# One scale for each head pair of batch 0, a weight bound from maxima, and two results moved from PSUM to SBUF, with the instruction order laid anew

## The chip, the cores and the metric

The kernel runs on one core of one Trainium2 chip. The metric is the time of one execution on the device, in microseconds. Five engines of the core appear here: PE (TensorE, the matrix engine; PEld are its weight loads), DVE (VectorE), ACT (ScalarE), POOL (GpSimd) and SP (SyncE, which here only starts DMA transfers). Each engine works through its own instructions strictly in the order of the program; the engines wait for one another by semaphores. SBUF is the on-chip memory that all engines and the DMA engines reach; matmuls write to PSUM.

## The reference

Eight batches, each of 576 tokens, go through three stages. Stage 1 is attention over 8 heads of 64, masked by blocks of 64 tokens. Stage 2 is a mixture of four attention experts, of which each token takes two. Stage 3 is a gated MLP that mixes tokens with a 576 x 576 matrix.

```python
scores = q @ k.T / 8;  scores = where(block_i >= block_j, scores, -1e9)
attn = exp(scores - max);  attn = attn / (sum(attn) + 1e-9)
x = concat_heads(attn @ v)                              # 8 x 576 x 512, fp32

logits = x @ w_gate;  topk, w = two best of 4, softmax of their logits
for e in range(4):                                      # causal attention of each expert
    ye = softmax(causal(x @ wq[e] @ (x @ wk[e]).T / 8)) @ (x @ wv[e]) @ wo[e]
    out += where(e in topk, w_e, 0) * ye

h = relu(out @ w_in);  u, v = halves of h (512 each)
v_n = (v - mean) / sqrt(var + 1e-6)
result = (u * (w_spatial @ v_n + b_spatial)) @ w_out
```

All inputs are fp32. The kernel keeps fp32 accuracy with 16-bit matmuls: every operand is scaled by a power of two, split into a high and a low fp16 part, and each product is three matmuls (high x high, high x low, low x high).

## The kernel before

**Tiles and steps.** Heads are taken in pairs: four pairs per batch in stage 1 and two pairs of experts (numbers 4 and 5) in stage 2, so 48 pairs in all. Everything that belongs to a pair or a batch is cut into *steps*, and each step into pieces that run on one engine each. For a pair of stage 1: the loads of q and k, and of v, into a buffer `nat` (load_qk, load_v); the maxima of their absolute values (mags, L279 or L281); the transposes and the split into fp16 (prep_qk L320, split16 L227 and L233; prep_v). One scale per batch comes from the maxima of all four pairs (scale1, scale2; col_max L195, bcast L206, scales L213 to L222). For every pair: four blocks of scores (matmuls L369, last block L384), each followed by the row maximum (L391, L393), a small step that makes the bias of the exponential from it (L401 on ScalarE or L403 on VectorE), and the exponential (L407, L412). The exponentials of blocks 0 to 2 land in SBUF buffers `pf`; that of the last block, 576 columns, is written back into its own PSUM buffer. Then the weights are split: a 16-bit copy (L327, L329 or L331) and a subtraction (L431) that gives the low part. They are transposed by three DMA transposes (L438, weights_t), and attention x V follows (av, L448). Its result is divided by the row sums (L464 to L466) and multiplied in place in PSUM (L471); a cast (L480 or L482) and a subtraction (L484), both from PSUM, give its two 16-bit halves `xh`, which a DMA transposes (L486).

The six pairs of a batch feed the dense part: projections (proj L803), vproj (L826), gate, then the two expert pairs, then hv (L882), norm (L920 to L926), gating (L961), gating2 (L977 to L985) and outp (L997, L1000).

**Buffers.** PSUM is four buffers called `duo`, 1024 fp32 columns each, and every step that uses TensorE takes one. A buffer comes free when the last piece that reads it is done. `pf` has three buffers, `nat` four.

**Startup.** Beside batch 0 the weights are prepared. w_in and w_out come as 64-bit words (s_win, s_wout, conversion L511 to L531) and are split (s_hl L714, L716). Of wq, wk and wv a bound on their column sums is taken: absolute values on ScalarE (L597), then 16 fp32 matmuls with a matrix of ones (s_abm, L626). The constants that follow from it (s_cons, L633 to L656) are needed before the dense part, and the steps of all weights of a pair wait for that bound. w_spatial is loaded into the buffers `pT` and transposed from there (L675).

**What sets the order.** Nothing is scheduled at run time. A list of numbers, ORDER, says which step runs its next piece, and a table, WAYS, says on which engine a piece runs that several engines can do ("AG": copy on ScalarE, subtraction on GpSimd). A piece may only come after the pieces it depends on and after its buffers are free, and each engine then meets its instructions in the order of the list.

## Time and profile before

| | |
|---|---|
| median of 3 runs | 1085.67 us (1085.58, 1085.67, 1089.9) |
| span of the profiled execution | 1086.0 us |
| TensorE busy | 894.5 us (82%) |
| VectorE busy | 832.3 us (77%) |
| ScalarE busy | 666.3 us (61%) |
| GpSimd busy | 374.6 us (34%) |
| DMA queue 1, which SyncE starts | 134.03 MB, 67.2% of 16 engines' span |

The profile is that of one execution. Each engine has a line that says how long it was busy; "idle before" an instruction is the time in which its engine had nothing to run, and the name behind the arrow is what ended it. PEclk is the clock that was granted to TensorE, as a share of its full 2.4 GHz; the DMA share is the mean busy share of the core's 16 DMA engines.

### The profile page before, as it was taken

Reading aid. Unit: us, or ns where it says so; the run is one execution under the profiler, and the core shown is the slowest. Engines: PE = TensorE matmul, PEld = TensorE weight load, DVE = VectorE, ACT = ScalarE, POOL = GpSimd, SP = SyncE. Lnnn points to the kernel's source line nnn. Section 1 sums busy time; section 2 is a strip of 40 time slices with the busy share of each in tenths; the row PEclk is TensorE's granted clock in tenths of the full one; section 3 lists DMA queues with packets and bytes.
Section 4 is the critical chain, followed back from the end, with each engine's and each line's share of the span. In section 5 each row is a group of like instructions: output and inputs, shape, how many; then the busy total and the mean of one; then the engine's idle time right before and its main releaser. Section 6 shows DMA issues by size and latency. Waiting matters only on the chain.

```text
span 1086.0 us, 25340 instructions
## 1 busy us (share of the span) xinstructions
PE 894.5 (82%) x10170; PEld 649.8 (60%) x10170; DVE 832.3 (77%) x1719; ACT 666.3 (61%) x1154; POOL 374.6 (34%) x307
## 2 busy tenths in 40 slices
PE   0477677777889799599999888987999999999978
PEld 0255555656567467466676556755777677667644
DVE  2698889898976868877897889877987887657550
ACT  2758467586677646666567657865667774636432
POOL 5145504152154212343244414354564044305000
PEclk9968687988989899799999998998999999999989
DMA  9536989798379678559649994959968546923601
GB/s 221 135 84 142 188 150 179 147 163 148 80 128 177 132 146 158 105 116 184 129 94 172 177 171 97 163 118 200 142 103 138 131 70 113 191 61 55 130 8 44
DMA packets 496663, 143.68 MB, mean 132 GB/s; under 512 B 484288, under 2 KB 490608, under 8 KB 496544
## 3 DMA queue, kind: packets, MB, share of 16 engines
q1 hardware_dynamic: 483744, 134.03, 67.2%
q0 software_dynamic: 2336, 5.55, 1.9%
q10 hardware_dynamic: 10464, 2.47, 1.4%
q8 instruction: 80, 1.31, 0.5%
q14 instruction: 39, 0.32, 0.1%
HBM read 38.19 MB, written 9.44 MB: 44 GB/s over the span
## 4 chain that ended last, share of the span: by engine, by line
PE 33%; DVE 14%; DMA 7%; ACT 6%; issue 4%; SPq 2%; POOL 1%; DVEq 0%; ACTq 0%; POOLq 0%
PE duo L977 7%; PE duo L997 6%; PE duo L448 5%; DMA pT<-p 5%; PE duo L803 4%; PE duo L369 3%; ACT pf L412 2%; PE duo L961 2%; DVE st L391 2%; PE duo L882 2%; PE duo L826 2%; PE duo L320 1%; DMA nat<-in_k_dram 1%; PE duo L384 1%; DMA nat<-in_v_dram 1%
## 5 line engine op out<-in xcount | busy, mean ns | idle before, releaser
L431 POOL TENSOR_TENSOR p<-pf,p 128x1024 f16<-128x1024 f32 (+1 forms) x96 | 187.3, 1954 | 326.3 <-ACT p L327 217.2
L412 ACT ACTIVATE pf<-duo,st,es 128x128 f32<-128x128 f32 (+3 forms) x256 | 139.3, 621 | 65.0 <-DVE st L403 48.1
L448 PEld LDWEIGHTS <-pT 128*128 128x128 f16 x4320 | 151.4, 101 | 29.9 <-issue 12.1
L391 DVE TENSOR_REDUCE st<-duo 128x2 f32<-128x1024 f32 (+1 forms) x192 | 150.8, 813 | 14.6 <-PE duo L377 8.4
L369 PE MATMUL duo<-qk 64*128 64x256 f16 (+3 forms) x1152 | 117.6, 321 | 29.7 <-ACT pf L412 14.0
L977 PE MATMUL duo<-wsp,vn 128*128 128x288 f16 x896 | 121.7, 290 | 11.2 <-ACT vn L923 5.5
L448 PE MATMUL duo<-v,pT 128*128 128x65 f16 (+1 forms) x2880 | 108.9, 200 | 15.0 <-DMA pT<-p 7.1
L997 PE MATMUL duo<-wo,gT 128*128 128x512 f16 (+1 forms) x480 | 109.2, 383 | 8.5 <-DVE xh L484 3.9
L977 PEld LDWEIGHTS <-vn 128*128 128x128 f16 x896 | 87.1, 99 | 36.2 <-ACT vn L923 6.1
L803 PE MATMUL duo<-x,wqk 128*128 128x288 f16 x768 | 102.4, 294 | 5.6 <-ACT pf L412 2.0
L803 PEld LDWEIGHTS <-wqk 128*128 128x128 f16 x768 | 76.2, 100 | 27.8 <-issue 6.3
L369 PEld LDWEIGHTS <-qk 64*128 64x128 f16 x1152 | 49.9, 99 | 62.1 <-issue 44.0
L997 PEld LDWEIGHTS <-gT 128*128 128x128 f16 (+1 forms) x480 | 47.2, 101 | 62.5 <-issue 12.3
L281 DVE TENSOR_REDUCE mst<-nat 128x1 f32<-128x640 f32 (+1 forms) x52 | 55.4, 1069 | 35.5 <-DMA nat<-in_v_dram 26.8
L412 ACT ACTIVATE pf<-duo,st,mt 128x384 f32<-128x384 f32 (+3 forms) x128 | 69.9, 616 | 15.0 <-DVE st L403 12.1
L331 POOL TENSOR_SCALAR p<-pf 128x1024 f16<-128x1024 f32 (+1 forms) x36 | 36.5, 1014 | 117.3 <-DMA pT<-p 62.6
L327 ACT CAST p<-pf 128x1024 f16<-128x1024 f32 (+1 forms) x71 | 66.5, 947 | 9.1 <-DMA pT<-p 7.1
L320 PE MATMUL duo<-ident,nat 128*128 128x128 f32 (+1 forms) x320 | 56.4, 314 | 17.1 <-DVE xh L484 6.4
L826 PE MATMUL duo<-wvg,x 128*128 128x260 f16 x480 | 57.6, 278 | 11.6 <-DVE st L403 5.8
L233 DVE SCALAR_TENSOR_TENSOR qk<-duo,scb,qk 128x640 f16<-128x640 f32 (+1 forms) x64 | 52.7, 843 | 18.4 <-ACT qk L227 18.2
L227 ACT ACTIVATE qk<-duo,scb 128x640 f16<-128x640 f32 (+1 forms) x64 | 47.8, 769 | 25.9 <-PE duo L320 15.9
L384 PE MATMUL duo<-qk 128*128 128x288 f16 x288 | 47.6, 303 | 17.5 <-ACT pf L412 13.2
(257 smaller groups left out, 1740.1 us busy)
## 6 DMA issues: line engine op xcount, KB each, us to landing
out_dram<-o SPq DMA_DIRECT2D x16, 512.0 KB, 3.3
nat<-in_q_dram SPq DMA_DIRECT2D x54, 128.0 KB, 3.1
nat<-in_k_dram SPq DMA_DIRECT2D x54, 128.0 KB, 3.1
nat<-in_v_dram SPq DMA_DIRECT2D x54, 128.0 KB, 3.1
wf<-in_moe_w_in_dram SPq DMA_DIRECT2D x8, 512.0 KB, 4.6
pT<-p SPq DMA_TRANSPOSE x144, 4.9
wf<-in_moe_w_out_dram SPq DMA_DIRECT2D x4, 512.0 KB, 4.9
nat<-in_q_dram POOLq DMA_DIRECT2D x10, 128.0 KB, 4.6
```

What stands on the lines that cost most here:

```text
L320: T.transpose(ps[:, P * c:P * c + r], p.nat[0:r, i, c, :], ident[0:r, 0:r])
L327: A.copy(hi, src)
L369: T.matmul(ph[:, hh, o:o + w], p.q[hs, a, ts], p.k[hs, bb, 0:w], start=i == 0, stop=False)
L384: T.matmul(ps[:, MID + a:MID + a + n], p.q[:, l, 512:640], p.k[:, r, a:a + n], start=i == 0, stop=i == 2 and not (p.moe and a))
L391: V.reduce_max(st[:, 0, 2 * c:2 * c + 2], ph[:, :, off[c]:off[c] + P * (c + 1)], axis=AX.X)
L412: A.activation(pf[:, n * hh + off[c]:n * hh + off[c] + w], ph[:, hh, off[c]:off[c] + w], AF.Exp, bias=st[:, 1, 2 * c + hh:2 * c + hh + 1], ...
L431: (V if way[1] == "D" else G).tensor_sub(lo, src, hi)
L448: T.matmul(ps[:, hh, o:o + n], pT[:, col(t, kk):col(t, kk) + P], p.v[:, hh, kk, a:a + n], start=kk == 0 and i == 0, stop=kk == nk - 1 and ...
L803: T.matmul(ps[:, MID + a:MID + a + w], wqk16[:, l, c, 2 * n + i, :], x16[c][:, r, a:a + w], start=m == 0, stop=m == 11)
L826: T.matmul(ps[:, i, :260], x16[d][:, l, P * c:P * c + P], wvg16[:, r, d, :], start=m == 0, stop=m == 11)
L977: T.matmul(ps[:, MID + a:MID + a + n], vn[:, l, ds_], wsp16[:, r, c, a:a + n], start=i == 0, stop=False)
L997: T.matmul(ps[0:r, i], gT[:, x, d, P * c:P * c + r], wo16[:, y, d, :], start=m == 0, stop=m == 11)
```

## The change

- **Start.** The buffers `nat` are made first, and GpSimd's first instruction clears the part of them that no load fills. The table of the exponential is loaded on ScalarE by one dummy instruction. The padding of `p16` and `pT` is cleared once, so one small matmul per pair (before at the end of scores) goes.
- **Batch 0** takes a scale of its own for each head pair (scale0, and scale2 with n = 2), from that pair's q and k alone; v still has one scale per batch.
- **Weight bound.** Absolute values and the matmuls of s_abm go; the bound comes from the largest element of the weights (s_mxA), which the scale of the weights needs in any case. The weights steps of pairs no longer wait for it. w_spatial is loaded into tiles of its own.
- **Last exponential** goes to a fourth `pf` buffer in SBUF, and its PSUM buffer is free after it. Copy and subtraction of that block read SBUF and may run on any engine.
- **Attention output** is multiplied from PSUM into a `pf` buffer (halves, first piece), and PSUM is free after that. Cast and subtraction read SBUF; the subtraction may run on GpSimd.
- **Attention x V** starts with the first of the three transposes and waits for each as it comes to it.
- **ORDER and WAYS** are new. All conversions and splits of w_in and w_out run on GpSimd, more bias steps on ScalarE, 40 of 48 subtractions of the attention output on GpSimd; of the 48 subtractions of the last block 37 stay on VectorE.

```diff
-BIG = -1.0e38
+BIG = -1.0e35
...
+    nat_t = buffers("nat", 4, 3 * NC * P).rearrange("p n (i c d) -> p n i c d", i=3, c=NC)
+    G.memset(nat_t[:, 0, :, 4], 0.0)
...
-    buffers("pf", 3, 1024)
+    buffers("pf", 4, 1024)
...
+    A.activation(junk[:, 0:1], ones[:, 0:1], AF.Exp)
...
+    def scale0(b, pr):
+        s = BS[b].own[pr]
+        s.dg = yield from col_max(duo(), s.st[:, :, 0], 2, "o")
...
     def prep_qk(b, pr, i):
         p, s = PD[b, pr], BS[b]
+        if b == 0:
+            s = s.own[pr]
...
-            T.matmul(ps[:, MID + S:MID + 640], identb, m_row[:, 64:128], start=True, stop=True)
...
-            A.activation(ps[:, MID:MID + S], ps[:, MID:MID + S], AF.Exp, bias=st[:, 1, 8:9], scale=p.es)
+            A.activation(pf[:, 0:S], ps[:, MID:MID + S], AF.Exp, bias=st[:, 1, 8:9], scale=p.es)
...
-        V.tensor_mul(ov[:, :, :, 0:64], ov[:, :, :, 0:64], r.unsqueeze(3).to_broadcast([P, 2, NC, D]))
-        p.x32 = ov[:, :, :, 0:64]
+        p.ov, p.r = ov[:, :, :, 0:64], r
     def halves(p, way):
...
-        if way == "A":
-            A.copy(hh, p.x32)
-        else:
-            V.tensor_copy(hh, p.x32)
-        yield
-        V.tensor_sub(hl, p.x32, hh)
+        x = mine("pf")[:, 0:640]
+        V.tensor_mul(x.rearrange("p (c h d) -> p h c d", h=2, c=NC), p.ov,
+                     p.r.unsqueeze(3).to_broadcast([P, 2, NC, D]))
+        yield
+        copy16(h[:, 0], x, way[0])
+        yield
+        (V if way[1] == "D" else G).tensor_sub(h[:, 1], x, h[:, 0])
...
-        def s_absA():
-            A.activation(t["aqk"], t["wqk"].rearrange("p c g i e d -> p c (g i e d)"), AF.Abs, accum_out=t["st"][:, 0:1])
...
+        def s_mxA(i):
+            V.tensor_reduce(t["st"][:, i:i + 1], (t["wqk"].rearrange("p c g i e d -> p (c g i e d)"),
+                                                  t["wv"].rearrange("p c e d -> p (c e d)"))[i],
+                            op=OP.max, axis=AX.X, apply_absolute_value=True)
...
-        def s_abm(i):
-            for c in range(KD):
-                T.matmul(pb[:, :n], ones, t[a][:, c, :], start=c == 0, stop=c == KD - 1)
-            V.reduce_max(t["amax"][:, i:i + 1], pb[:, :n], axis=AX.X)
...
     ORDER = (
...
-        "su.win.0": ("D",), "su.hl.0": ("D",), "su.win.1": ("G",), "su.hl.1": ("G",), "su.win.2": ("D",),
+        "su.win.0": ("G",), "su.win.1": ("G",), "su.win.2": ("G",), "su.win.3": ("G",), "su.win.4": ("G",),
...
+        "x.0": ("AG", "AG", "AG", "AG", "AG", "GD", "AG", "GD"), "x.1": ("AG", "AG", "DG", "AD", "AG"),
```

Three places show how the instructions move. The first is TensorE at the start of the program. Before, in a row (`p` holds absolute values of weights, `wst` and `m` maxima, L320 transposes the first pair's q):

```order
L626 MATMUL duo<-p_140,ones 128x256 x4
L626 MATMUL duo<-p_140,ones 128x512 x4
L195 MATMUL duo<-ident,m_318 3x128
L195 MATMUL duo<-ident,wst 5x128
L700 MATMUL duo<-ident,V_144 128x128 x8
L206 MATMUL duo<-dgb,ones 128x3
L206 MATMUL duo<-dgw,ones 128x5
L320 MATMUL duo<-ident,nat 128x128 x9
L320 MATMUL duo<-ident,nat 128x64
```

After, the same engine from its first instruction to its first scores:

```order
L199 MATMUL duo<-ident,mst_217 2x128
L210 MATMUL duo<-dgo,ones 128x2
L343 MATMUL duo<-ident,nat 128x128 x9
L343 MATMUL duo<-ident,nat 128x64
L389 LDWEIGHTS qk
L389 MATMUL duo<-qk 128x512
```

The weight bound, the weights' scale and w_o's transposes no longer stand ahead of the first pair; two small matmuls of the pair's own scale do.

The second place is VectorE in the middle of the program, at the end of a pair's attention. Before (`rr` is the reciprocal of the row sums, `xh` the halves of the attention output, L980 a step of the gated MLP):

```order
L464 TENSOR_SCALAR rr<-duo 128x10
L466 RECIPROCAL rr<-rr 128x10
L471 TENSOR_TENSOR duo<-duo,rr 128x2x5x64
L484 TENSOR_TENSOR xh<-duo,xh 128x2x5x64
L980 TENSOR_TENSOR u<-duo,u 128x576
```

After, at such a place:

```order
L480 TENSOR_SCALAR rr<-duo 128x10
L482 RECIPROCAL rr<-rr 128x10
L485 TENSOR_TENSOR rr<-rr,wt 128x10
L410 TENSOR_REDUCE st<-duo 128x2 x3
L493 TENSOR_TENSOR pf<-duo,rr 128x2x5x64
L448 TENSOR_TENSOR p_144<-pf,p_144 128x1024
L352 CAST p_144<-pf 128x1024
```

The subtraction has left VectorE here, and the multiplication is what frees the PSUM buffer.

The third place is GpSimd, where those subtractions (L498) now stand among the weights' (L448), after:

```order
L448 TENSOR_TENSOR p_144<-pf,p_144 128x1024 x2
L498 TENSOR_TENSOR xh<-pf,xh 128x640
L448 TENSOR_TENSOR p_144<-pf,p_144 128x1024
L498 TENSOR_TENSOR xh<-pf,xh 128x640
L448 TENSOR_TENSOR p_144<-pf,p_144 128x1024
L354 TENSOR_SCALAR xh<-pf 128x640
L448 TENSOR_TENSOR p_144<-pf,p_144 128x1024
L498 TENSOR_TENSOR xh<-pf,xh 128x640
```

Before, GpSimd had no instruction on `xh`; now a weight subtraction stands ahead of most of them.

## Rows read from the trace of the kernel before

**Rows 1.** Busy time, share of the span and instruction count of each engine.
```profile
PE 894.5 (82%) x10170; PEld 649.8 (60%) x10170; DVE 832.3 (77%) x1719; ACT 666.3 (61%) x1154; POOL 374.6 (34%) x307
```

**Rows 2.** Stretches: length, each engine's busy time (instructions), PEclk, DMA share, GB/s.
```profile
0.00:66.00 66.00, 18.55 (x71) 12.26 (x72) 33.97 (x97) 33.22 (x58) 27.06 (x52) 0.90 0.77 166
66.00:240.00 174.00, 124.19 (x1445) 97.79 (x1446) 157.35 (x278) 116.58 (x211) 62.95 (x42) 0.79 0.82 152
240.00:955.00 715.00, 635.13 (x7708) 462.92 (x7703) 574.85 (x1189) 465.32 (x801) 265.30 (x196) 0.96 0.76 139
955.00:1086.00 131.00, 116.64 (x956) 76.87 (x953) 66.11 (x156) 51.20 (x85) 19.32 (x17) 0.94 0.24 53
...
100.00:140.00 40.00, 26.81 (x324) 22.85 (x323) 34.13 (x54) 23.74 (x43) 18.41 (x11) 0.70 0.91 159
850.00:900.00 50.00, 48.41 (x475) 35.07 (x474) 41.64 (x99) 36.75 (x70) 13.29 (x12) 1.00 0.49 94
```

**Rows 3.** Timeline of PE: start, length, instruction, in brackets the idle time before it.
```profile
36.69 8.19 PE L626 MATMUL duo<-p,ones 128*128 128x256 f32 x16 [36.69 <-ACT p L597]
...
65.99 1.64 PE L369 MATMUL duo<-qk 64*128 64x512 f16 x6
...
240.42 0.91 PE L384 MATMUL duo<-qk 128*128 128x288 f16 x6
...
954.90 1.39 PE L803 MATMUL duo<-x,wqk 128*128 128x288 f16 x5
```

**Rows 4.** Timeline of POOL, SP (its DMA issues) and ACT at the start.
```profile
5.28 1.49 POOL L162 MEMSET nat<- 128x384 f32 x4
...
9.22 1.21 SPq L254 DMA_DIRECT2D nat<-in_q_dram  x2
10.47 0.66 SPq L256 DMA_DIRECT2D nat<-in_k_dram  x1
...
17.33 1.28 ACT L279 ACT_TABLE_LOAD   x1 [17.33 <-DMA nat<-in_k_dram]
```

**Rows 5.** Waits of PE, 240 to 955 us: engine, line, releaser; total us, times, longest.
```profile
PE duo L384 <- ACT pf L412: 8.1, 6, 3.7
PE duo L320 <- DVE xh L484: 6.4, 2, 3.8
...
PE duo L997 <- DVE xh L484: 3.9, 1, 3.9
...
PE duo L448 <- DVE xh L484: 2.1, 2, 1.1
...
PE duo L206 <- ACT pf L412: 0.5, 1, 0.5
```

**Rows 6.** DVE groups, 0 to 240 us: instruction, shape, count; busy us, mean ns; idle before.
```profile
L431 DVE TENSOR_TENSOR p<-pf,p 128x1024 f16<-128x1024 f32 x9 | 12.1, 1349 | 1.9 <-POOL p L331 1.9
...
L281 DVE TENSOR_REDUCE mst<-nat 128x2 f32<-128x1280 f32 x5 | 7.4, 1485 | 1.2 <-DMA nat<-in_k_dram 1.1
...
L484 DVE TENSOR_TENSOR xh<-duo,xh 128x640 f16<-128x640 f32 x7 | 5.7, 813 | 0.0
...
L530 DVE TENSOR_TENSOR x<-x,e 128x512 f32<-128x512 f32 x5 | 3.4, 685 | 0.1
...
L403 DVE TENSOR_SCALAR st<-st,es 128x2 f32<-128x2 f32 x9 | 2.3, 255 | 0.0
```

**Rows 7.** Single lines over the span: count, shortest/median/longest in ns, first to last, shapes.
```profile
L431 DVE TENSOR_TENSOR p<-duo,p x48: 802/815/825, 84.6 to 1010.8; 128x640 f16<-128x640 f32 x48
...
L985 DVE TENSOR_TENSOR gT<-u,gT x13: 744/749/2203, 343.1 to 1069.4; 128x576 f16<-128x576 f32 x13
...
L431 POOL TENSOR_TENSOR p<-pf,p x96: 1150/2128/3186, 76.3 to 998.9; 128x1024 f16<-128x1024 f32 x72, 128x512 f16<-128x512 f32 x24
```

**Rows 8.** ACT groups over the whole span, columns as in rows 6.
```profile
L480 ACT CAST xh<-duo 128x640 f16<-128x640 f32 x44 | 30.6, 695 | 25.1 <-DVE duo L471 15.7 <-PE duo L379 4.3 <-issue 2.9
...
L401 ACT ACTIVATE st<-st,ln,es 128x2 f32<-128x2 f32 x20 | 7.7, 387 | 18.1 <-DVE st L391 18.1
```

More of the change, by code (lines that the diff above doesn't have):

```diff
@@ L101, in attn_moe_gmlp_kernel @@
     onesb = cst.tile([P, P], BF, name="onesb")
+    for n in range(1, 4):
+        G.memset(nat_t[:, n, :, 4], 0.0)
     G.memset(onesb, 1.0)
@@ L160, in attn_moe_gmlp_kernel @@
     junk = cst.tile([P, 640], BF, name="junk")
-    for n in range(4):
-        G.memset(nat_t[:, n, :, 4], 0.0)
     for n in range(3):
@@ L353, in scores @@
             p.st = sm.tile([P, 2, 9], F32, name="st")
[L354 to L358 removed]
+            p.pf, p.p16, p.pT = {}, {}, {}
+        pf = p.pf[j] = mine("pf")
         st = p.st
@@ L424, in weights @@
             p.p16[g] = mine("p16")
-        s0, n, o0, per = WCOL[j]
-        src = p.pf[j][:, s0:s0 + n] if j < 3 else p.last[:, s0:s0 + n]
+        n, o0, per = WCOL[j]
+        src = p.pf[j][:, 0:n]
         t = p.p16[g]
@@ L1370, in pair_steps @@
         for j in range(4):
[L1371 to L1375 removed]
+            n = (1024, 1024, 512, 576)[j]
```

162 lines of the change are left out of this document (80 added, 82 removed), and 475 rows, old and new, of tables (ORDER, WAYS).

## The prediction

> **What bounds the kernel now.** I read the busy times first [rows 1]. TensorE is busy for 894.5 us of 1086.0, VectorE for 832.3, ScalarE for 666.3, GpSimd for 374.6: no engine is full, so the question is where TensorE waits. The stretches of [rows 2] answer it. The borders are points that the reordered program passes too: 66 us is the first score matmul, 240 us the last score block of batch 0's second expert pair, 955 us the first projection of batch 7 [rows 3]. In the first 66 us TensorE works for 18.6 us. From 66 to 240 it works for 124.2 of 174, at a granted clock of 0.79, and VectorE is busy for 157.4, that is 90%: VectorE sets the pace there. The DMA share is 0.82, so it is second. From 240 to 955 TensorE works for 635.1 of 715 at clock 0.96, and VectorE for 574.9 (80%): TensorE leads, with 79.9 us of idle time. The last 131 us are batch 7's own chain, with no other batch left beside it.
>
> So there are three terms: the start (240), the middle (715), the end (131). They add up to the span of 1086.0; the median of the runs is 1085.67, so nothing is added for time outside the span.
>
> **The start.** Before, the last small load of the first pair is issued at 10.47 us, because the loads into that buffer wait for a memset that stands behind the mask work on GpSimd (5.28, 1.49 us long); its data is there at 17.33 [rows 4]. Scaling needs the maxima of all four pairs. In front of everything else on TensorE stands the weight-bound matmul, 8.19 us, which waits until 36.69 for ScalarE, and the first score comes at 65.99 [rows 3].
>
> After, the memset is GpSimd's first work, and the scale comes from the pair's own q and k. SyncE needs about 4 us for its seven issues (the two in one row of [rows 4] are 1.21 us together). The last issue of before landed 6.9 us later (10.47 to 17.33) in a crowded queue; 4 us seems fair with fewer loads ahead, so the first maximum starts at about 9 us (8 to 12). The maximum (1.485 us [rows 6]), five small steps between VectorE and TensorE, two blocks of transposes and two splits put the first score at about 16 us. That is 50 us earlier, but not 50 us gained: the work of VectorE and of the DMA engines remains.
>
> VectorE worked for 33.97 + 157.35 = 191.3 us up to the 240 us point. Up to the same point the new order changes this, with durations from [rows 6]:
> - seven subtractions of the attention output go to GpSimd: 7 x 0.813 = -5.7;
> - six conversion blocks of weights, two steps of like width each, go to GpSimd: 12 x 0.685 = -8.2, and three more subtractions of weights: -2.1;
> - nine 1024-wide weight subtractions become three: 6 x 1.349 = -8.1;
> - 12 of 18 small bias steps go to ScalarE: 12 x 0.255 = -3.1;
> - the maxima of q and k: five on VectorE become twelve, 7 x 1.485 = +10.4;
> - four scales of single pairs, nine small steps each, at 0.2 (they are smaller than the 0.255 of a bias step, which gives the upper end of 9): +7; the weight bound from maxima, 3072 elements at 1.485/1280: +3.6;
> - fewer 512-wide subtractions and casts, an estimate between -3 and -10: -7.
>
> The sum is -13.2, so 178.1 us remain, of which some 8 are constants before 9 us. The other 170 at the 90% of [rows 2] take 188, plus 9, plus 7 us in which VectorE waits for the first pair: **204 us**. The DMA engines check this: 0.77 x 66 + 0.82 x 174 = 193.5 us of their time, and the same loads and transposes are due by then. At a share of 1.0 they need 194, at 0.91 (100 to 140 us [rows 2]) 213. Bounds: 190 and 222. I take the value from VectorE, since 0.91 was reached in a stretch of before that VectorE paced too (34.13 of 40).
>
> **The middle.** Two PSUM buffers are released earlier for each pair: that of the last score block after its exponential, where a cast (0.695) and a subtraction (0.815) followed, and that of the attention output after one multiplication, where another cast and subtraction followed [rows 7, 8]. That is at least 2 x 1.51 = 3.0 us for each of 48 pairs, of 4 buffers x 1086 us: 3.3%. Against it, attention x V now starts when the first of three transposes has landed, and its buffer is held while the others come: 0 to about 6 us more per pair. So that trade lies on both sides of nothing. TensorE's waits [rows 5] say what is to be had: 6.4 + 3.9 + 2.1 = 12.4 us were waits for the very subtraction that reads the attention output out of PSUM; these go. Waits named for an exponential make 17.7 us in seven lines (the first and the last are shown); half, 9, as they stand for a score block that comes late. Fewer gaps raise the clock: it was 0.96 here and 1.00 in the densest 50 us; half way, 635.1 x 0.96 / 0.98 = 622, -13. Sum -34: **681 us**, with bounds of 715 (all given back) and 630 (the pace of 850 to 900 us, 48.41 of 50 at clock 1.00: 635.1 x 0.96 / 0.968).
>
> Cover: the new work on GpSimd in the whole program is 40 subtractions 640 wide at about 2.128 x 640/1024 = 1.33 [rows 7], 53 us, and with the weights' blocks it goes from 374.6 to about 455; it still has 58% of the span free, so this costs nothing unless TensorE waits for a particular one (rival 4). ScalarE takes 85 more bias steps of 0.387 [rows 8], +33; it has 39% free [rows 1], and these steps stand between a maximum and its exponential, so if ScalarE is late they cost 0.387 - 0.255 = 0.13 us of a pair's chain, which other pairs cover.
>
> **The end.** TensorE's steps from 955 on are the same in the same order; 131 becomes **130** (126 to 134).
>
> Total: 204 + 681 + 130 = **1015 us**.
>
> **A rule against it.** VectorE's subtraction out of PSUM never varied (802 to 825 ns), while a VectorE step with both inputs in SBUF goes from 744 to 2203, and GpSimd's from 1150 to 3186 [rows 7]. 45 subtractions that stay on VectorE change from the first kind to the second. By the rows' medians (749 against 815) they cost nothing; if each were held up to the longest, 45 x (2.203 - 0.749) = 65 us of VectorE. The Trainium skill (SBUF — State Buffer, Who interferes with whom) says that a VectorE instruction with two SBUF inputs contends with a GpSimd instruction that reads SBUF, and that whoever comes second waits for the other's whole length. By that rule the longest is the price to expect where both are dense, which leads to rival 1.
>
> **Rivals.**
> 1. *Only the start gains.* The held buffer of attention x V, and VectorE held up at those 45 places, eat the middle's 34 us: 204 + 715 + 130 = 1049. For it: 80 us of new GpSimd work beside VectorE. Against: 12.4 us of waits are named for instructions that no longer hold PSUM. Chance 0.22.
> 2. *Dense throughout.* The start takes 190 and the middle runs at the pace of its best 50 us: 190 + 630 + 128 = 948. For it: VectorE is at 83% in that stretch, so no engine stops it. Against: the stretch had light DMA traffic (0.49). Chance 0.14.
> 3. *The start stays bound by transfers.* If the DMA engines reach only 0.85, the point comes at 193.5/0.85 = 228, with waits for transposes: 228 + 681 + 131 = 1040. Chance 0.08, inside the range.
> 4. *Slower: GpSimd in order.* The subtraction behind each attention output now queues on GpSimd behind weight subtractions of 2.13 us median, 3.19 at most [rows 7]. Per pair the path to the transposes of x grows from 0.82 to 1.33 plus such a wait, by up to 1.33 + 3.19 - 0.82 = 3.7 us. If TensorE had nothing else to do then, 48 x 3.7 = 178 us, and 1015 + 178 = 1193; it decides from (1086 - 1015)/48 = 1.5 us exposed per pair. Against: TensorE has another batch's steps at hand. Chance 0.04.
> 5. *It does not do what it says*: the new order is a fixed list, made for durations that the chip may not keep, and the queues stall each other by as much as is gained: 1086. Chance 0.03.
>
> **How the numbers follow.** The forecast has 0.49; its own bounds are 975 and 1045. With rivals 1 and 3 inside and half of 2 below, the range is 968 to 1052. A measurement of this kernel tells about 0.5% (5 us) from no change. Faster: 0.49 + 0.22 + 0.14 + 0.08 = 0.93; within: 0.03; slower: 0.04.
>
> **What would show it.** First score between 14 and 20 us; batch 0's last expert score block between 190 and 222; VectorE near 780 us busy and GpSimd near 455; no wait of TensorE named for the subtraction of the attention output; granted clock above 0.85 before that block. I am wrong if TensorE's idle time in the middle stays near 80 us, if GpSimd's subtraction of the attention output ends waits of projections, or if the DMA share of the start is above 0.95 with TensorE waiting for transposes.

## The result and the profile after

The changed kernel takes 1055.54 us (median, 1052.95 to 1056.75) beside 1086.32 us for the kernel before: a ratio of 0.9699 with a 95% interval of 0.9671 to 0.9728, 3.0% faster. The forecast was 1015 us with a range of 968 to 1052, so the direction held, the gain was less than half of what was forecast, and the time lies 3.5 us outside the range.

The profiled execution has a span of 1053.8 us. The busy times, as [rows 1]:

```profile
PE 902.1 (86%) x10118; PEld 654.3 (62%) x10118; DVE 791.7 (75%) x1616; ACT 669.8 (64%) x1206; POOL 469.6 (45%) x394
```

VectorE has 41 us less to do, GpSimd 95 us more; TensorE is busy for 7.6 us *longer* than before. The timeline of TensorE gives the points of [rows 3]: the first scores, the last score block of batch 0's second expert pair, the first projection of batch 7.

```profile
24.23 0.61 PE L389 MATMUL duo<-qk 64*128 64x512 f16 x2 [10.32 <-ACT qk L232]
...
226.03 0.91 PE L404 MATMUL duo<-qk 128*128 128x288 f16 x6
...
924.58 9.69 PE L804 MATMUL duo<-x,wqk 128*128 128x288 f16 x72
```

So the terms are 226.0 (forecast 204, before 240.4), 698.6 (681, before 714.5) and 129.2 (130, before 131.1). The stretches between these points, as [rows 2]:

```profile
0.00:24.20 24.20, 3.33 (x13) 2.64 (x14) 10.21 (x48) 2.91 (x4) 11.57 (x34) 1.00 1.02 220
24.20:226.00 201.80, 137.45 (x1493) 104.37 (x1492) 179.55 (x324) 142.47 (x255) 121.00 (x95) 0.80 0.76 155
...
226.00:924.60 698.60, 643.74 (x7664) 470.17 (x7662) 538.75 (x1088) 473.25 (x862) 313.90 (x250) 0.96 0.77 143
924.60:1053.80 129.20, 117.55 (x953) 77.13 (x952) 63.19 (x158) 51.16 (x85) 23.14 (x16) 0.95 0.24 54
```

Three readings follow. From the first scores on VectorE is busy for 179.55 of 201.80 us, 89%: the pace that the forecast took from [rows 2] held. But VectorE has 10.21 + 179.55 = 189.8 us to do up to that point, where 178.1 were forecast. And in the middle TensorE's idle time fell from 79.9 to 54.9 us, while its busy time rose from 635.1 to 643.7 at the same clock of 0.96.

**Where the first pair stood.** Its maximum began at 8.23 us, as forecast (9), and its transposes were on TensorE at 11.43. ScalarE's timeline shows why the scores came only at 24.2. The DMA issues are those with ACTq, and the length of a row runs from its first start to its last end, waits between them included:

```profile
6.92 2.05 ACTq L579 DMA_DIRECT2D x<-in_moe_wk_dram  x4
9.47 8.19 ACTq L583 DMA_DIRECT2D x<-in_moe_wv_dram  x4
22.26 0.39 ACTq L586 DMA_DIRECT2D wg<-in_moe_w_gate_dram  x1
22.76 1.42 ACT L232 ACTIVATE qk<-duo,sco 128x640 f16<-128x640 f32 x2 [20.47 <-DMA nat<-in_k_dram]
```

ScalarE starts the loads of the weights, and the first pair's split, L232, is queued behind those of wv and of the gate's weights. (The arrow of L232 names a load of k; what the split reads, the transposes of L343, was done at 13.9.) The issues themselves are short (shortest/median/longest in ns):

```profile
L583 ACTq DMA_DIRECT2D x<-in_moe_wv_dram x4: 374/374/375, 9.5 to 17.3; - x4
```

What takes the time is the wait ahead of each. In the trace every issue names a semaphore that its transfer raises when it lands. Eight semaphores serve the transfers of SyncE and ScalarE together, eight others those of GpSimd, each in turn; of the 555 issues whose semaphore had been used before, none starts until the earlier transfer on it has landed. So the fourth issue for wv starts at 17.29 us, behind the landing of wk's last load at 17.26, and the issue for the gate's weights at 22.26, behind a load of q that SyncE had issued at 10.76 and that landed at 22.24. With the DMA engines at a share of 1.02 (the first stretch above), wv's loads took 7.4 to 12.6 us from issue to landing. SyncE's issues for the next pairs are held in the same way; its own view of waits names the load (total us, times, longest):

```profile
14.52 8.01 SPq L259 DMA_DIRECT2D nat<-in_q_dram  x2
...
SPq L259 <- DMA x<-in_moe_wv_dram: 5.0, 1, 5.0
```

**TensorE's waits in the middle**, as [rows 5]:

```profile
PE duo L464 <- ACT pf L431: 6.9, 4, 2.4
...
PE duo L343 <- ACT pf L431: 5.3, 4, 2.6
...
PE duo L343 <- DVE pf L493: 1.3, 1, 1.3
```

No wait is named for a subtraction of the attention output any more; the multiplication that now frees PSUM (L493) ends 2.0 us in four lines. But the waits for exponentials, 17.7 us in [rows 5], are 22.4 us in seven lines.

### The profile page after: what moved, and what is told of

Read it like the earlier page. It is cut to its first block, busy times and chain, and to the rows that moved or that the text cites. A ratio compares the mean times of both kernels' runs of the same rounds, so it can differ in the third digit from the quotient of the medians.

```text
span 1053.8 us, 25324 instructions
## 1 busy us (share of the span) xinstructions
PE 902.1 (86%) x10118; PEld 654.3 (62%) x10118; DVE 791.7 (75%) x1616; ACT 669.8 (64%) x1206; POOL 469.6 (45%) x394
## 4 chain that ended last, share of the span: by engine, by line
PE 46%; DVE 10%; ACT 5%; issue 2%; DMA 1%; ACTq 0%; SPq 0%; POOL 0%; DVEq 0%; POOLq 0%
PE duo L978 9%; PE duo L464 8%; PE duo L998 8%; PE duo L804 5%; PE duo L883 4%; PE duo L962 3%; PE duo L389 3%; DVE st L410 3%; PE duo L827 2%; ACT pf L431 2%; PE duo L404 2%; PE duo L343 1%; DVE qk L238 1%; DVE p L448 1%; ACT vn L924 1%
## 5 line engine op out<-in xcount | busy, mean ns | idle before, releaser
L448 POOL TENSOR_TENSOR p<-pf,p 128x1024 f16<-128x1024 f32 (+2 forms) x111 | 201.1, 1818 | 172.8 <-ACT p L350 74.4
L464 PEld LDWEIGHTS <-pT 128*128 128x128 f16 (+1 forms) x4320 | 159.6, 102 | 44.6 <-issue 23.4
L410 DVE TENSOR_REDUCE st<-duo 128x2 f32<-128x1024 f32 (+2 forms) x192 | 150.3, 816 | 36.4 <-PE duo L399 22.3
L464 PE MATMUL duo<-v,pT 128*128 128x65 f16 (+3 forms) x2880 | 117.0, 200 | 16.7 <-ACT pf L431 10.6
L431 ACT ACTIVATE pf<-duo,st,es 128x512 f32<-128x512 f32 (+3 forms) x224 | 122.0, 617 | 10.4 <-DVE rr L485 3.7
L498 POOL TENSOR_TENSOR xh<-pf,xh 128x640 f16<-128x640 f32 x40 | 57.6, 1439 | 121.4 <-ACT xh L350 115.5
L448 DVE TENSOR_TENSOR p<-pf,p 128x576 f16<-128x576 f32 (+2 forms) x81 | 83.3, 1034 | 15.2 <-ACT p L350 9.2
L350 ACT CAST p<-pf 128x1024 f16<-128x1024 f32 (+2 forms) x104 | 82.6, 809 | 1.2 <-DMA pT<-p 0.2
L354 POOL TENSOR_SCALAR p<-pf 128x1024 f16<-128x1024 f32 (+2 forms) x46 | 42.7, 928 | 88.8 <-ACT pf L431 47.8
L343 PE MATMUL duo<-ident,nat 128*128 128x128 f32 x320 | 58.4, 319 | 18.3 <-ACT pf L431 6.1
L431 ACT ACTIVATE pf<-duo,st,mt 128x256 f32<-128x256 f32 (+3 forms) x128 | 69.9, 616 | 5.7 <-DVE st L422 4.3
L404 PE MATMUL duo<-qk 128*128 128x288 f16 x288 | 50.5, 318 | 20.1 <-ACT pf L431 15.2
```

Source lines behind the costliest of these rows:

```text
L343: T.transpose(ps[:, P * c:P * c + r], p.nat[0:r, i, c, :], ident[0:r, 0:r])
L350: A.copy(hi, src)
L404: T.matmul(ps[:, MID + a:MID + a + n], p.q[:, l, 512:640], p.k[:, r, a:a + n], start=i == 0, stop=i == 2 and not (p.moe and a))
L410: V.reduce_max(st[:, 0, 2 * c:2 * c + 2], ph[:, :, off[c]:off[c] + P * (c + 1)], axis=AX.X)
L431: A.activation(pf[:, n * hh + off[c]:n * hh + off[c] + w], ph[:, hh, off[c]:off[c] + w], AF.Exp, bias=st[:, 1, 2 * c + hh:2 * c + hh + 1], ...
L448: (V if way[1] == "D" else G).tensor_sub(lo, src, hi)
```

## Experiments

Medians and the ratios to the kernel before, with their 95% intervals. The kernel before ran beside each group of experiments, with medians of 1086.2 to 1090.2 us; so a difference of up to 4 us between medians of different groups says little, and the ratios decide.

### Rows of the last chunk

One detail of the change stands neither in the shortened diff nor in the forecast: the last 64 tokens of a pair are now multiplied with 64 rows of V, and not with 128 rows of which 64 hold zeros.

```diff
-                r = P if kk < 4 else 64
+                r = P
```

> The changed kernel, with the last chunk of attention x V read over all 128 rows again instead of 64 (the rows behind 64 hold zeros, so the sums stay the same). Theory: the middle missed its forecast because every change between 128 and 64 rows lays one weight load open; in the trace of the changed kernel the matmuls of such a chunk follow 119 ns after the one before, where 29 to 33 ns are usual, three to four times per pair. 48 pairs x 3 to 4 x 0.09 us = 13 to 17 us: 1039 to 1043 us, TensorE's busy time on the line of attention x V back from 117.0 to about 109 us. Rival: TensorE is busier because the three pieces of attention x V now run apart, one behind each transpose; then nothing changes, 1053 to 1058 us.

1048.56 us, ratio 0.9660 (0.9627 to 0.9692). And the reverse, in the kernel before:

```diff
+                r = P if kk < 4 else 64
-                    T.matmul(ps[:, hh, o:o + n], pT[:, col(t, kk):col(t, kk) + P], p.v[:, hh, kk, a:a + n],
+                    T.matmul(ps[:, hh, o:o + n], pT[0:r, col(t, kk):col(t, kk) + P], p.v[0:r, hh, kk, a:a + n],
```

> The kernel before, with one part of the change alone: the last chunk of attention x V read over 64 rows. Theory of the changes between row counts: 13 to 17 us slower, 1099 to 1103 us (somewhat less where TensorE waited anyway). Rival (pieces that run apart): they stay together here, so nothing changes, 1084 to 1090 us.

1092.52 us, ratio 1.0061 (1.0039 to 1.0083). The costliest groups show attention x V on TensorE (busy us, mean ns; idle time before); first the changed kernel, stage 1 and expert pairs:

```profile
L464 PE MATMUL duo<-v,pT 128*128 128x65 f16 (+3 forms) x2880 | 117.0, 200 | 16.7 <-ACT pf L431 10.6 <-DVE woT L706 1.5 <-DVE qk L238 1.5
L464 PE MATMUL duo<-V,pT 128*128 128x65 f16 (+2 forms) x1440 | 57.9, 199 | 10.5 <-DMA pT<-p 5.2 <-ACT pf L426 3.0 <-ACT pf L431 2.2
```

then e1_rows128:

```profile
L464 PE MATMUL duo<-v,pT 128*128 128x65 f16 (+1 forms) x2880 | 107.0, 200 | 18.1 <-ACT pf L431 11.0 <-DMA pT<-p 2.5 <-DVE woT L706 1.5
L464 PE MATMUL duo<-V,pT 128*128 128x65 f16 (+1 forms) x1440 | 55.4, 202 | 11.0 <-DMA pT<-p 5.8 <-ACT pf L426 2.9 <-ACT pf L431 2.2
```

174.9 us become 162.4 with the same number of matmuls, and all of TensorE goes from 902.1 to 889.8 busy. With 64 rows in the kernel before, these lines go from 108.9 + 51.6 to 119.7 + 55.5 us, 14.7 more. So the price of changing between 64 and 128 rows is 0.26 to 0.31 us of TensorE per pair, 13 to 15 us in all, as expected, and the rival (pieces that run apart) is out. The trace of the changed kernel shows it at the changes alone: the median step from one matmul's start to the next is 124 ns where 64 rows follow 128 and 120 ns back, and 29 to 39 ns within either kind. The time, though, moved by only 7.0 and 6.3 us (0.4% and 0.6% by the ratios), and both expectations of the time were missed. The stretches of e1_rows128 between the three points, as [rows 2]:

```profile
0.00:227.05 227.05, 138.52 (x1506) 105.53 (x1507) 188.82 (x371) 145.42 (x259) 133.33 (x129) 0.77 0.80 162
227.05:920.05 693.00, 635.76 (x7666) 463.81 (x7663) 536.99 (x1088) 473.41 (x862) 314.54 (x250) 0.95 0.78 144
```

Of TensorE's 12.3 us, 8.0 went in the middle, which got 5.6 us shorter, since its idle time rose a little (57.2 us against 54.9). 2.3 went in the start, whose end came 1.0 us *later*: VectorE sets the pace there.

### The first pair behind the weights' loads

The changed kernel, with the last five of ScalarE's weight loads behind the first pair's exponentials (85 is its last score step), and VectorE's maxima of weights (3, 4) ahead of step 5:

```diff
+    for i in [i for i, x in enumerate(ORDER) if x == 1][8:][::-1]:
+        del ORDER[i]
+    ORDER.remove(3)
+    ORDER.remove(4)
+    i = [i for i, x in enumerate(ORDER) if x == 85][-1] + 1
+    ORDER[i:i] = [1] * 5
+    i = ORDER.index(5)
+    ORDER[i:i] = [3, 4]
...
-    sua("ldwo", 31, [("POOL", 0.75, 0.35)], ["ldA"])
+    sua("ldwo", 31, [("POOL", 0.75, 0.35)], ["open"])
```

The last line lets w_o's load go ahead without these five.

> The changed kernel, with the loads of wv and of the gate's weights (five issues on ScalarE), and the two maxima of weights on VectorE, moved behind the first pair's exponentials. Theory: the first scores came at 24.2 us and not at 16, because ScalarE stood in its own issues of those loads (8.19 us for four of them, the last at 22.26) when the first pair's transposes were done at 13.9. First scores at 16 to 17.5 us, and the time 4 to 7 us lower, 1048.5 to 1051.5. Rival: the VectorE work up to batch 0's last expert scores sets that point, so what the first pair gains is lost to the next ones: first scores earlier, but 1053.5 to 1057.5 us.

1060.65 us, ratio 0.9761 (0.9726 to 0.9795): both expectations missed; it is slower than the changed kernel (0.9699). The first scores came at 14.7 us, and then TensorE's waits say

```profile
PE duo L210 <- DVE eso L324: 12.6, 1, 12.6
```

The second pair's scale stood on VectorE behind the maximum of wv, and that behind wv's load, which now came late. The maxima were moved back to where they are used:

```diff
-    i = ORDER.index(5)
+    i = ORDER.index(6)
```

> As e2_late_wv, with the two maxima of weights on VectorE moved further back, to the place where the weights' scale is taken from them. In e2_late_wv the first pair's scores began at 14.7 us, but TensorE then waited 12.6 us for the second pair's scale, since VectorE stood at the maximum of wv, whose load came late. Theory: the first pair's gain of 9.5 us carries now, as nothing of the weights stands ahead of the pairs: 1047 to 1050.5 us. Rival: VectorE's whole work sets batch 0 (it is busy for 89% from the first scores on), and what the pairs gain, the weights' constants lose behind them: batch 0's last expert scores within 3 us of 226, time 1053 to 1057.5 us.

1063.22 us, ratio 0.9783 (0.9748 to 0.9818): missed again. The first scores came at 15.2, and the second pair waits, this time on ScalarE:

```profile
31.56 5.50 ACTq L583 DMA_DIRECT2D x<-in_moe_wv_dram  x4
39.91 0.37 ACTq L586 DMA_DIRECT2D wg<-in_moe_w_gate_dram  x1
40.33 1.19 ACT L350 CAST p<-pf 128x512 f16<-128x512 f32 x2 [12.40 <-DMA wf<-in_moe_w_in_dram]
```

with TensorE at

```profile
46.78 0.61 PE L389 MATMUL duo<-qk 64*128 64x512 f16 x2 [13.40 <-ACT qk L232]
```

The waits are of the same kind: the issue at 39.91 stands behind the landing, at 39.89, of a load of w_in on the same semaphore, which SyncE had started at 32.7. So these issues hold ScalarE at both places that were tried. They were then given to GpSimd, at the places that they have in the changed kernel (on top of e1_rows128):

```diff
-                A.dma_start(t["wv"][:, :, e, :], wv[e].rearrange("(c p) d -> p c d", p=P))
+                G.dma_start(t["wv"][:, :, e, :], wv[e].rearrange("(c p) d -> p c d", p=P))
...
-            A.dma_start(t["wg"], w_gate.rearrange("(c p) e -> p c e", p=P))
+            G.dma_start(t["wg"], w_gate.rearrange("(c p) e -> p c e", p=P))
```

> As e1_rows128 (1048.6 us), with the five loads of wv and of the gate's weights started by GpSimd instead of ScalarE, at the same places of the order. In e2_late_wv and e5_late_wv_max those issues held ScalarE wherever they stood (in e5_late_wv_max from 31.6 to 39.9 us, and the second pair's split waited for that). Theory: ScalarE is then free when the first pair's transposes are done at 13.9, first scores at 15 to 17, the second pair no later than in the changed kernel (44.8), 2 to 7 us faster: 1041.5 to 1046.5. Rival: the DMA engines are full up to 23 us (share 0.99 and more), so the second pair's loads and everything behind come as before: first scores earlier, time within 2 us of 1048.6.

**1041.24 us**, ratio 0.9553 (0.9527 to 0.9579), 7.3 us below e1_rows128 (0.9660) by the medians and the lowest of all: the theory held, just beyond its end. On GpSimd's semaphores nothing was outstanding yet. It issues the four loads in 3.22 us, 0.75 to 0.97 us each and without a wait, and TensorE's timeline begins

```profile
15.73 0.61 PE L389 MATMUL duo<-qk 64*128 64x512 f16 x2 [0.83 <-ACT qk L232]
21.22 1.04 PE L389 MATMUL duo<-qk 64*128 64x512 f16 x4 [4.87 <-DVE qk L238]
```

The point of batch 0's last expert scores comes at 222.2 instead of 227.1: the 4.9 us that the first pair's score block gained (its row maxima began at 22.9 and not 27.8) are still there after 200 us. The middle is 3.1 us shorter too (689.9 for 693.0), which this experiment does not explain. What was left of the first pair's delay is on VectorE, which waits for the load of wk:

```profile
16.81 2.29 DVE L613 TENSOR_REDUCE wst<-x 128x1 f32<-128x2048 f32 x1 [3.40 <-DMA x<-in_moe_wk_dram]
```

So these maxima were moved as in e2_late_wv, now with early loads:

```diff
+    ORDER.remove(3)
+    ORDER.remove(4)
+    i = ORDER.index(5)
+    ORDER[i:i] = [3, 4]
```

> As e9_wv_pool (1041.2 us), with VectorE's two maxima of weights moved behind the first pair's scores. In e9_wv_pool the first scores came at 15.7, but their second half waited 4.87 us for VectorE, which stood at the maximum of the weights and so at the load of wk. Theory: in-order waits on the weights are all that delayed the first pair; what it gains is carried on by the pairs behind it, as the 4.5 us of e9_wv_pool were: 3 to 6 us faster, 1035 to 1038 us. Rival: VectorE's whole work sets the point now, since the maxima stand in the second pair's way instead: 1040 to 1046 us.

1043.11 us, ratio 0.9586 (0.9559 to 0.9612): no gain, as the rival had it. The first pair's row maxima come 5.0 us earlier still, the second pair's 1.1 us *later* than in e9_wv_pool. TensorE's first waits for the next pairs are for the maxima of their q and k, and the maxima of the weights now stand on VectorE ahead of the second pair's scale:

```profile
PE duo L199 <- DVE mst L295: 10.8, 2, 7.5
...
34.30 3.40 DVE L613 TENSOR_REDUCE wst<-x 128x1 f32<-128x2048 f32 x2
```

So only the first pair gains, and the second gives it back.

### VectorE beside GpSimd

The nine steps of the weights' conversion and split that VectorE had before, on VectorE again:

```diff
+    WAYS.update({"su.win.0": ("D",), "su.hl.0": ("D",), "su.win.2": ("D",), "su.hl.2": ("D",), "su.win.3": ("D",), "su.win.5": ("D",), "su.win.7": ("D",), "su.hl.7": ("D",), "su.wout.3": ("D",)})
```

> The changed kernel, with the nine steps of the conversion and split of w_in and w_out that were on VectorE before the change (six conversions, three subtractions) on VectorE again instead of GpSimd. Theory: VectorE was busy for 189.8 us up to batch 0's last expert scores instead of the forecast 178.1, because GpSimd's longer work there (132.6 us against 90.0) lengthens VectorE's other steps by some 14 us. With these steps back VectorE gets their own 10.3 us, and its other steps lose 5 to 9 us of that lengthening, so VectorE's busy time there is 191 to 195 us and the time within -2 to +5 us, 1053 to 1060. Rival: the durations have nothing to do with GpSimd; VectorE's busy time there rises by all of 10.3 us to 200, and the time by 10 to 12 us, to 1066.

1055.29 us, ratio 0.9723 (0.9695 to 0.9751), the changed kernel's time. Up to the end of batch 0's last expert scores, here and in the changed kernel (columns as in [rows 2]):

```profile
0.00:230.60 230.60, 136.99 (x1513) 105.43 (x1514) 194.43 (x392) 146.06 (x261) 117.28 (x114) 0.79 0.79 159
```
```profile
0.00:226.80 226.80, 141.58 (x1513) 107.64 (x1514) 190.52 (x377) 145.97 (x261) 133.01 (x129) 0.82 0.79 162
```

VectorE has 15 instructions more and 3.9 us more work, not the 10.3 at which the forecast priced these steps: the other 6.4 us are steps that got shorter. That is the theory, in its range. The point itself came 3.8 us later, and the time did not: the middle gave them back, so the three terms of the forecast are not independent here.

Both SBUF results, each alone in the kernel before. First the attention output:

```diff
+    buffers("xp", 3, 640)
-        V.tensor_mul(ov[:, :, :, 0:64], ov[:, :, :, 0:64], r.unsqueeze(3).to_broadcast([P, 2, NC, D]))
-        p.x32 = ov[:, :, :, 0:64]
+        p.x32 = mine("xp").rearrange("p (c h d) -> p h c d", h=2, c=NC)
+        V.tensor_mul(p.x32, ov[:, :, :, 0:64], r.unsqueeze(3).to_broadcast([P, 2, NC, D]))
```

> The kernel before, with one part of the change alone: the attention output is multiplied from PSUM into SBUF buffers of its own (three of 640), cast and subtraction read these, and the PSUM buffer is free after the multiplication; order and engines as before. Theory of the prediction: TensorE's 12.4 us of waits for that subtraction in the middle, and 1.7 at the start, go: 8 to 14 us faster, 1072 to 1078 us. Rival: another releaser stands right behind them (the next exponential or transpose), so little is gained: 1083 to 1088 us.

1098.59 us, ratio 1.0096 (1.0069 to 1.0122): slower. The subtraction in the kernel before, and here (shortest/median/longest in ns):

```profile
L484 DVE TENSOR_TENSOR xh<-duo,xh x48: 805/818/826, 108.7 to 1023.1; 128x640 f16<-128x640 f32 x48
```
```profile
L485 DVE TENSOR_TENSOR xh<-xp,xh x48: 807/824/5180, 108.6 to 1037.0; 128x640 f16<-128x640 f32 x48
...
L485 DVE TENSOR_TENSOR xh<-xp,xh 128x640 f16<-128x640 f32 x48 | 60.2, 1253 | 21.9 <-ACT xh L481 21.7
```

The median is the same, the longest is 5.18 us, and the 48 take 60.2 us where 39.3 were spent. The traces show where the long ones stand. One of them, with GpSimd's step beside it, and the same pair in the kernel before:

```profile
341.80 2.29 DVE L485 TENSOR_TENSOR xh<-xp,xh 128x640 f16<-128x640 f32 x1 [2.18 <-ACT xh L481]
341.27 2.13 POOL L432 TENSOR_TENSOR p<-pf,p 128x1024 f16<-128x1024 f32 x1 [6.36 <-issue]
```
```profile
339.94 0.82 DVE L484 TENSOR_TENSOR xh<-duo,xh 128x640 f16<-128x640 f32 x1 [2.15 <-ACT xh L480]
339.44 2.14 POOL L431 TENSOR_TENSOR p<-pf,p 128x1024 f16<-128x1024 f32 x1 [6.03 <-ACT p L327]
```

Out of SBUF the subtraction ends 0.68 us behind the end of GpSimd's step, out of PSUM it runs through beside it. All of them go this way: 14 of the 48 here took over 0.83 us (1.1 to 5.2); each began inside a step of GpSimd and ended 0.67 to 0.76 us behind the end of one. Of the other 34 one began inside such a step, which had 0.06 us left. In the kernel before 17 of the 48 began inside one, and none took over 0.83. Then the last exponential:

```diff
+    pl_t = buffers("pl", 2, 640)
-            p.last = ps
+            p.last = mine("pl")
-            A.activation(ps[:, MID:MID + S], ps[:, MID:MID + S], AF.Exp, bias=st[:, 1, 8:9], scale=p.es)
+            A.activation(p.last[:, 0:S], ps[:, MID:MID + S], AF.Exp, bias=st[:, 1, 8:9], scale=p.es)
```

> The kernel before, with one other part alone: the last block's exponential goes to SBUF buffers of its own (two of 640), copy and subtraction read these, and its PSUM buffer is free after the exponential; order and engines as before. Theory of the prediction: half of TensorE's 17.7 us of waits for exponentials in the middle go, 5 to 9 us faster: 1077 to 1081 us. Rival: those waits stand for an exponential that comes late on ScalarE, not for a missing buffer: 1083 to 1089 us.

1095.97 us, ratio 1.0080 (1.0049 to 1.0111), slower too. Here the 48 subtractions of the last block, 0.815 us each out of PSUM [rows 7], became

```profile
L433 DVE TENSOR_TENSOR p<-pl,p 128x640 f16<-128x640 f32 x48 | 51.1, 1064 | 5.7 <-ACT p L329 4.5 <-POOL vf L922 0.7 <-issue 0.2
```

Again 14 of the 48 took over 0.83 us; each began inside a step of GpSimd and ended 0.68 to 0.76 us behind the end of one, and none of the other 34 began inside one. Both runs miss both of their expectations. That the longer subtractions make all of the 8 to 11 us is not shown.

With the attention output's subtraction on GpSimd instead, on top of e6_before_x_sbuf:

```diff
-        V.tensor_sub(hl, p.x32, hh)
+        G.tensor_sub(hl, p.x32, hh)
```

> As e6_before_x_sbuf (the kernel before, attention output multiplied into SBUF, 1098.6 us), with all 48 subtractions of the attention output on GpSimd instead of VectorE. Theory: e6_before_x_sbuf lost because that subtraction, with both inputs in SBUF, took VectorE 60.2 us instead of 39.3; without it VectorE is free of all of that, and the early release of PSUM shows what it is worth: 6 to 15 us faster than before, 1072 to 1081 us. Rival: GpSimd in order (the forecast's fourth rival): the subtraction stands behind weight subtractions of 2.1 us, the transposes of x come later, and TensorE waits for them: 1086 to 1099 us.

1108.01 us, ratio 1.0167 (1.0143 to 1.0191): the rival, and beyond it. VectorE's busy time fell from 859.5 to 822.7 us, but SyncE, which starts the transposes of x and of the weights in one queue, waited in the middle for GpSimd. Its waits for that subtraction in the kernel before, and here:

```profile
SPq L486 <- DVE xh L484: 12.8, 4, 9.5
```
```profile
SPq L487 <- POOL xh L485: 60.6, 15, 12.3
```

That this held queue is what costs the time is the likely reading; TensorE's waits do not name it.

In the changed kernel's own order the same choice costs nothing that these runs show. e1_rows128 with all subtractions of the attention output on VectorE:

```diff
-        "x.2": ("AG", "AG", "AG", "AG", "AG", "AG", "AG", "GD"), "x.3": ("AG", "AG", "AD", "AG"),
+        "x.2": ("AD", "AD", "AD", "AD", "AD", "AD", "AD", "GD"), "x.3": ("AD", "AD", "AD", "AD"),
...
```

> As e1_rows128 (1048.6 us), with the 40 subtractions of the attention output that run on GpSimd moved to VectorE, in the changed kernel's order. Theory: VectorE gets 40 subtractions with both inputs in SBUF, at the 1.25 us that they took in e6_before_x_sbuf 50 us of work, and loses some 57 us of GpSimd's that held it up; 8 to 25 us slower, 1057 to 1074 us. Rival (the forecast's fourth): GpSimd's queue makes x late in the changed kernel, and VectorE, which is faster at it, takes nothing away that counts: 1040 to 1049 us.

1053.72 us, ratio 0.9674 (0.9655 to 0.9692), 5 us above e1_rows128 by the medians, but of another group: the two ratios (0.9674, 0.9660) lie within each other's intervals. The 8 to 25 us of the theory did not come. The 48 took 42.7 us on VectorE, 891 ns each and not 1253: here only 5 of them took over 0.83 us, against 14 in e6_before_x_sbuf, since fewer began inside a step of GpSimd.

### Bias steps

e1_rows128 with the bias steps on the engines of the kernel before (24 entries, of which three are shown):

```diff
+    WAYS.update({"sc.0.0": ("D", "D", "D", "D", "D", "D", "D", "A"),
+        "sc.0.1": ("D", "A", "A", "D", "D", "D", "D", "A"),
...
+        "sc.5.3": ("A", "A", "D", "D", "D", "D", "D", "A")})
```

> As e1_rows128 (the changed kernel with 128 rows in the last chunk, 1048.6 us), with the small bias steps of the exponentials on the engines of the kernel before, so 85 more of them on VectorE and as many fewer on ScalarE. Theory: exponentials end 22.4 us of TensorE's waits in the middle of the changed kernel, more than the 17.7 before, because ScalarE carries those steps: 3 to 8 us faster, 1041 to 1046 us. Rival: VectorE, which gets some 85 x 0.3 = 25 us of work back, sets the pace in the start and its maxima come later: 1054 to 1061 us.

1068.85 us, ratio 0.9825 (0.9793 to 0.9857): 20 us slower than e1_rows128, as the rival had it and more, but not where it saw it: the end of the start moved by 2.9 us (229.9 for 227.1), and the middle by 15.9 (708.9 for 693.0). VectorE's busy time rises by 20.7 us to 809.6. The two commonest shapes of these small steps over the whole span, in the kernel before and here:

```profile
L403 DVE TENSOR_SCALAR st<-st,es 128x2 f32<-128x2 f32 x44 | 15.3, 349 | 0.2
L403 DVE TENSOR_SCALAR st<-st,mt 128x2 f32<-128x2 f32 x23 | 9.0, 390 | 0.1
```
```profile
L422 DVE TENSOR_SCALAR st<-st,es 128x2 f32<-128x2 f32 x40 | 18.9, 472 | 0.1
L422 DVE TENSOR_SCALAR st<-st,mt 128x2 f32<-128x2 f32 x23 | 13.8, 601 | 0.1
```

Of all 126, 28 took over 0.35 us here, and 26 of these began inside a step of GpSimd; in the kernel before 15 did, 14 of them inside one.

The reverse, the kernel before with the changed kernel's engines for them (its 24 entries "sc.0.0" to "sc.5.3"):

```diff
+    WAYS.update({"sc.0.0": ('A', 'D', 'A'),
+        "sc.0.1": ('A',),
...
+        "sc.5.3": ('A', 'A', 'D', 'D', 'D', 'D', 'D', 'A')})
```

> The kernel before, with one part alone: the small bias steps of the exponentials on the engines of the changed kernel, so 85 of them move from VectorE to ScalarE; everything else, the order too, as before. Theory: these steps are what the change gains most by. On VectorE they took 39.7 us for 126, 0.315 each, up to 2 us when held up; the reverse edit cost e8_bias_dve 20 us. Time 8 to 20 us lower, 1066 to 1079 us. Rival: the old order is laid for them on VectorE, and on ScalarE they wait behind casts and exponentials: 1082 to 1092 us.

1087.05 us, ratio 0.9992 (0.9974 to 1.0010): nothing, although VectorE's busy time falls by 13.4 us to 818.9. And all remaining 41 on ScalarE, in e1_rows128 and on top of e13_wv_pool_max:

```diff
+    WAYS.update({f"sc.{n}.{j}": ("A",) for n in range(6) for j in range(4)})
```

> As e1_rows128 (1048.6 us), with the 41 bias steps that are still on VectorE moved to ScalarE too. Theory: VectorE's small steps are what costs, 85 of them cost 20 us in e8_bias_dve, so 41 more give 3 to 9 us: 1039.5 to 1045.5 us. Rival: ScalarE, whose exponentials already end most of TensorE's waits, becomes the one that is late: 1048 to 1056 us.

> As e13_wv_pool_max, with the 41 remaining bias steps on ScalarE too (worth 1 us alone, in e12_bias_all_act). Theory: the same as there, 0 to 3 us below e13_wv_pool_max. Rival: with the start shorter ScalarE is the late one: 1 to 4 us above it.

1047.62 us, ratio 0.9610 (0.9589 to 0.9630), and 1042.84 us, ratio 0.9575 (0.9556 to 0.9594): no difference from their bases that is clear of noise (1048.56 us at 0.9660, with an interval that touches the first one's, and 1043.11 at 0.9586). VectorE lost another 12.9 us in the first of these (776.0) and the time did not follow by as much.

## Why the prediction was wrong, point by point

**The end** was right (129.2 for 130), and so was the rough shape: faster, by a start and a middle of like size. Each of the two gave less than half of its forecast: 14.4 of 36 us, 15.9 of 34. The sum of the terms is a span, and every run here for which both are on record took 1.7 to 1.9 us longer than its span; the forecast put this at nothing.

**The start, first step that failed: the first scores at 16 us.** The working listed the first pair's own instructions and their durations, and those came out as written; it did not list what stands ahead of the pair's split on ScalarE. From 9.5 to 22.7 us ScalarE worked off five issues, for wv and the gate's weights, each of which waited for an earlier transfer to land; the split came 8.9 us after its input. e9_wv_pool shows this step by itself: with these issues on GpSimd the first scores came at 15.7, as forecast; of the 8.9 us by which that is earlier than in e1_rows128, 4.9 were left at the end of the start. e2_late_wv and e5_late_wv_max show that moving them later on ScalarE only hands a wait to the second pair.

**The start, second step: VectorE's 178.1 us.** It was 189.8, 11.7 more. By the forecast's own sum that is (189.8 - 8)/0.9 + 9 + 7 = 218, and with first scores at 24 instead of 16 it is the measured 226. The maxima came out as priced (13.8 us for 14.0 with the weights' bound), and so did the four pairs' own scales (6.6 for 7). Three other things did not: the conversions and splits of weights gave 4.3 us and not 10.3, the bias steps 1.2 and not 3.1 (one of the five left took 2.08 us), and the scale steps of the batches and the weights, which the sum left as they were, took some 4 us more. The counts were right or off by one; the duration of steps that stayed on VectorE rose. Two conversion steps before and after, up to the same point:

```profile
L519 DVE TENSOR_SCALAR e<-wf 128x512 uint16<-128x512 uint16 x12 | 5.7, 471 | 5.5 <-DMA wf<-in_moe_w_in_dram 4.8 <-DMA wf<-in_moe_w_out_dram 0.7
L520 DVE TENSOR_SCALAR wout<-wf 128x512 int32<-128x512 int32 x4 | 1.7, 418 | 0.0
```
```profile
L533 DVE TENSOR_SCALAR e<-wf 128x512 uint16<-128x512 uint16 x12 | 8.1, 674 | 0.3 <-DMA wf<-in_moe_w_in_dram 0.3
...
L534 DVE TENSOR_SCALAR wout<-wf 128x512 int32<-128x512 int32 x4 | 5.8, 1438 | 0.0
```

The same instruction on the same shape takes 1438 ns instead of 418, while GpSimd's work up to there grew from 90.0 to 132.6 us. Of the twelve steps of L534, four took over 0.43 us, and each of the four began inside a step of GpSimd and ended 0.28 us behind it. e3_conv_dve agrees: with GpSimd back at 117 us, VectorE's steps got 6.4 us shorter. The "cover" paragraph priced GpSimd's new work at nothing; it costs VectorE.

**The middle, waits.** The 12.4 us named for the subtraction went, as forecast (a fourth row, L384 with 1.4 us, makes them 13.8), and TensorE's idle time fell to 54.9 us, near the 59 that the forecast implies (681 - 622). But the halving of the waits for exponentials (-9) did not come: they rose by 4.7, and 15.9 us of other idle time fell in their place, so the agreement is luck. As a price for the early release of PSUM the working is not upheld: in the kernel before, each of the two releases alone made it slower by 0.8 to 1.0%.

**The middle, busy time: the step that failed.** The forecast let TensorE's 635.1 us shrink to 622 as the clock rises. It rose to 643.7, and these 21.7 us are more than what the middle missed (17.6). 8.6 of them are the rise itself: the chunks of 64 rows, which the forecast did not price at all, and without which e1_rows128 has 635.8. The other 13 are the clock: it stayed at 0.96 although the idle time fell by 25 us, and in the profile of e1_rows128 it was 0.95.

**The rule weighed against the change** was weighed wrongly. The forecast took the medians and so nothing for 45 subtractions with both inputs in SBUF. The runs show the median unchanged and the mean far above it: 818 to 1253 ns for one subtraction, 815 to 1064 for the other, by those that began inside a step of GpSimd and ended behind it. The Trainium skill (SBUF — State Buffer, Who interferes with whom) states that such a VectorE instruction contends with a GpSimd instruction that reads SBUF; these runs agree, with 20.9 and 12.0 us per 48 subtractions. In the changed kernel 37 subtractions of the last block stay on VectorE, at a mean of 969 ns for 576 columns.

**Rivals.** The result lies beside rival 1 (1049) in size but not in kind: the middle did gain. Rival 4 (GpSimd in order) is what happens in the old order (e11_before_x_pool, +1.7%, probably by way of SyncE's queue), and does not show in the new one (e15_x_dve). Rivals 2 and 3 did not occur: the clock stayed low, 0.82 up to the last expert scores where the forecast's sign was above 0.85, and the DMA share was 0.76 after the first scores. That the measured 226 lies beside rival 3's 228 is chance: TensorE waited for transposes for 1.4 us in that stretch.

**What stays open.** Which part gives the middle's 15.9 us is not shown. In the old order the two releases cost 8 to 11 us each, the bias steps give nothing; in the new order taking the bias steps back costs 20. Engines and order are laid for each other, so that a single part in the other's order is not that part's worth. A later release of PSUM in the new order was not tried, and neither were the parts of the start (the pairs' own scales, the weight bound, the early clearing of `nat`) one by one.

## What to carry to other kernels

Price a chain by the queues that it passes through: here the first pair's split was 9 us late behind DMA issues in its own engine's queue, each of which waited for another transfer to land, and giving these to an engine whose semaphores were free and for which nobody waited was worth 7 us (1048.6 to 1041.2). A VectorE step with both inputs in SBUF, and a small one beside a busy GpSimd, is priced by its mean and its longest in the rows, not by its median. And a row count or tile shape that changes inside a run of matmuls is an edit with a price, however little work it saves.

## What the runs showed of the hardware

- A DMA issue held its engine by waiting, not by its own length: four issues of 0.37 us kept ScalarE from 9.47 to 17.66 us, and a fifth until 22.65, each behind the landing of an earlier transfer on the semaphore that it takes over, while the DMA share was 1.02. GpSimd, with semaphores of its own, started the same four in 3.22 us, at 0.75 to 0.97 us each.
- A last chunk of 64 rows among chunks of 128 cost TensorE 0.26 to 0.31 us per pair, 13 to 15 us in all, for the same number of matmuls: the first matmul after a change came 120 to 124 ns after the one before, where 29 to 39 are usual.
- When the 64-row chunks went, TensorE's busy time fell by 12.3 us and the time by 7.0. The granted clock over the whole run does not tell the two kernels apart: 0.919 to 0.928 with them, 0.911 to 0.925 without.
- A VectorE subtraction with both inputs in SBUF that began inside a step of GpSimd ended 0.67 to 0.76 us behind the end of such a step (28 of 28 long ones in two runs) and took up to 5.18 us, six times its median. The one out of PSUM began inside one 17 times in 48 and never passed 0.83.
